# DeltaNet and Fourier mixing on one core: all rounds inverted in 16-token blocks that TensorE joins, MLP activations on ScalarE alone, and a rearranged start

## The chip, the cores and the metric

The kernel runs on one core of a Trainium2 chip. A core has a matrix engine (TensorE, PE in the profile; its weight loads are listed as PEld), a vector engine (VectorE, DVE), an activation engine (ScalarE, ACT), a general engine (GpSimd, POOL) and a queue engine that issues most of the DMAs (SyncE, SP). Matrix products land in PSUM, from which DVE or ACT must copy ("evict") them to SBUF. The metric is the device time of the kernel in microseconds (us).

## The reference

Two blocks, one after the other. The first is a delta rule recurrence over 768 tokens for 4 batches x 8 heads with 48 channels per head; the second mixes each batch's 768 x 384 matrix by a two-dimensional Fourier transform and sends it through a normalised MLP.

```python
k_n = k / (np.linalg.norm(k, axis=-1, keepdims=True) + 1e-06)
for t in range(S):
    kt, vt, bt = (k_n[:, :, t], v[:, :, t], beta[:, :, t, None])
    y[:, :, t] = np.einsum('bhd,bhde->bhe', q[:, :, t], state)
    v_old = np.einsum('bhde,bhd->bhe', state, kt)
    state = state + bt[:, :, :, None] * np.einsum('bhd,bhe->bhde', kt, vt - v_old)
...
x = y.transpose(0, 2, 1, 3).reshape(B, S, H * D)          # 4 x 768 x 384
mixed = np.real(np.fft.fft(np.fft.fft(x, axis=1), axis=2))
u = x + mixed
un = (u - mean(u)) / np.sqrt(var(u) + 1e-06)
out = u + np.maximum(un @ w_ch1, 0.0) @ w_ch2             # 384 -> 1536 -> 384
```

All inputs are float32.

## The kernel before, in words

**Groups, steps and rounds.** The tokens are cut into 24 groups of 128 (`g`; six to a batch), each of two chunks of 64. Inside a chunk the recurrence is turned into matrix products, for which a triangular matrix of the keys' inner products must be inverted. This is done in blocks of 32 tokens, for four groups at a time: a *round* `r` (`RL` = 4), six rounds in all, rounds 0 and 1 for the first eight groups.

**What is done for a group.** `pre_a(g)` transposes the keys and forms the inner products `G` (and `GX` between the two blocks of a chunk). `invert(r)` turns a round's `G` into the inverse: a transpose, a short chain on the diagonal (norms), then an elimination of 31 pairs of DVE instructions (`tmp`, L376, and `M`, L380) over the whole 32 x 32 block of all heads at once, and two more transposes (L383, L384). `pre_q(g)` transposes the queries and forms their products with the keys, masked (`LQ`). `pre_m(g)` joins the two 32-blocks of a chunk on TensorE (`px`, `py`) and makes `WT` and `U0`. `step(g, c)` then advances the recurrence by one chunk: TensorE product, DVE subtraction (`U`, L601), TensorE product, DVE addition (`S`, L620), and after the second chunk the output `x`.

**Two ways to invert.** Rounds 0 and 1 use `invert16`: DVE eliminates only inside 16-token blocks (15 pairs, L453 and L456), and `join(g)` adds the missing corner per group with two sets of small TensorE products. The first set (`py`) needs the untransposed corner of `G`, which POOL copies to `Gc` beforehand (L411); ACT scales it into `Y` (L477), the second set (`pm`) follows, and DVE adds it to the inverse and its transpose (L491). Rounds 2 to 5 use `invert`, without joins.

**After the recurrence.** `fourier(b)` folds the batch (`E`, `O`) and multiplies it by tables (`evt`, `odt`, `dtab`); `mlp(b)` normalises (`un`), transposes, and runs the two matrix products: twelve chunks `ph` of 256 tokens, each evicted to `hT` with a ReLU, alternately by ACT (L769) and DVE (L771), then `po`, added to `x` by DVE (L781) and stored.

**Order of the work.** The engines' order is written out by hand: each function is a generator, and the program advances them piece by piece (`advance`, `part`, `run`). In batch 0 everything is in line: keys of rounds 0 and 1, inversion 0, queries, first joins, then for each group the steps with the next groups' `pre_m`, `join` and `pre_q` in between, inversion 1 and the weights' conversion in pieces (`fill`). From batch 1 on, `run` goes round-robin over one step, the next group's `pre_q` and `pre_m`, the next round's `pre_a` or inversion (24 pieces per step, 6 per turn, in three steps of the eight of a round), and the MLP of the batch before (`side`). SP's queue is not ordered by hand; the framework orders it.

**Spins.** `spin(n)` issues `n` products of a zero tile with itself (`unread<-idle`, L206) that nobody reads. They keep TensorE at work between pieces; there are 80 of them, two records each in the profile.

**Loads.** SP issues nearly all loads. POOL issues those of K and V for groups 0 and 1 and of beta for rounds 0 and 1; ACT issues a table of masks (`pack`) and one group of keys. The Fourier tables are issued before the first join.

Of the kernel before, what the change touches and what calls it, by code (L numbers as in the profile page):

```python
# [9 lines left out]
F32 = mybir.dt.float32  # L10
# [14 lines left out]
def _consts(S, DM):  # L25
# [6 lines left out]
    upper = -1.0 * (p[:, None] % W >= V16)  # L32
    pack = np.concatenate([ident, su, blk, upper], axis=1)
# [27 lines left out]
def kernel(  # L61
# [121 lines left out]
    pack = const.tile([128, 128 + C + 3], F32, name="pack")  # L183
    w2 = const.tile([128, KF, DM], F32, name="w2")

    early = w2.rearrange("p c m -> p (c m)").rearrange("p (n h d) -> p n h d", h=8, d=64)
    nc.vector.memset(early[:, :, :, D:64], 0.0)
# [12 lines left out]
    idle = wk.tile([128, 128], F32, tag="LQ", bufs=2, name="idle")  # L200
    nc.vector.memset(idle, 0.0)  # L201
    unread = []

    def spin(n):
        for _ in range(n):
            nc.tensor.matmul(unread[0][:, 0:128], lhsT=idle, rhs=idle, start=True, stop=True,  # L206
                             skip_group_check=True)
    m_su = pack[:, 128:128 + C]
    m_blk = pack[:, 128 + C:128 + C + 2]
    m_upper = pack[:, 128 + C + 2:128 + C + 3]  # L210
# [116 lines left out]

    def invert(r):

        G = Gs.pop(r)  # L330
        A = wk.tile([128, W, W], F32, tag="A", bufs=2, name="A")
        M = wk.tile([128, W, W], F32, tag="x" if r == 1 else "M", bufs=2 if r == 1 else 1,
                    name="M")
        nc.gpsimd.memset(M, 0.0)
        nc.vector.transpose(A, G.rearrange("p m s -> p s m"))
        yield
        nrm = wk.tile([128, W], F32, tag="nrm", bufs=2, name="nrm")
        bn = wk.tile([128, W], F32, tag="bn", bufs=2, name="bn")
        flat = "p a b -> p (a b)"
        diag = A.rearrange(flat)[:, 0:W * W:W + 1]  # L340

        nc.scalar.activation(nrm, diag, ACT.Sqrt)
        yield
        nc.vector.tensor_scalar(nrm, nrm, 1e-19, None, op0=ALU.max)
        yield
        nc.vector.reciprocal(bn, nrm)
        yield
        nc.vector.tensor_tensor(bn, bn, diag, op=ALU.mult)
        yield
        nc.vector.tensor_tensor(nrm, nrm, bn, op=ALU.add)  # L350
        yield
        nc.vector.reciprocal(bn, nrm)
        yield
        nc.vector.tensor_tensor(bn, bn, diag, op=ALU.mult)
        yield
        nc.vector.scalar_tensor_tensor(nrm, nrm, 0.25, bn, op0=ALU.mult, op1=ALU.add)
        yield
        nc.vector.tensor_scalar(nrm, nrm, 1e-6, None, op0=ALU.add)
        yield
        nT = wk.tile([128, W], F32, tag="nT", bufs=2, name="nT")  # L360
        nc.vector.transpose(nT, nrm)
        nc.vector.tensor_tensor(nrm, nrm, nrm, op=ALU.mult)
        yield
        nc.vector.reciprocal(nrm, nrm)
        yield
        nc.vector.tensor_tensor(bn, nrm, betas.pop(r), op=ALU.mult)
        yield
        nc.vector.scalar_tensor_tensor(A, A, -1.0, bn[:, :, None].broadcast_to([128, W, W]),
                                       op0=ALU.mult, op1=ALU.mult)
        nc.vector.tensor_copy(M.rearrange(flat)[:, 0:W * W:W + 1], bn)  # L370
        yield
        for j in range(W - 1):
            n = W - 1 - j
            t = wk.tile([128, 256], F32, tag="tmp", bufs=2, name="tmp")
            t = t[:, 0:n * (j + 1)].rearrange("p (a b) -> p a b", a=n)
            nc.vector.tensor_tensor(t, A[:, j + 1:W, j:j + 1].broadcast_to([128, n, j + 1]),  # L376
                                    M[:, j:j + 1, 0:j + 1].broadcast_to([128, n, j + 1]),
                                    op=ALU.mult)
            yield
            nc.vector.tensor_tensor(M[:, j + 1:W, 0:j + 1], M[:, j + 1:W, 0:j + 1], t, op=ALU.add)  # L380
            yield

        nc.vector.transpose(A.rearrange("p m t -> p t m"), M)  # L383
        nc.vector.transpose(G.rearrange("p m s -> p s m"), M.rearrange("p t s -> p s t"))  # L384
        rounds[r] = (A, G, nT)
        yield

    Gc = {}

    def invert16(r):  # L390
# [3 lines left out]
        if not Gc:  # L394
            Gc[0] = wk.tile([128, 2, W, W], F32, tag="O", name="Gc")
# [10 lines left out]
        def pairs(t):  # L406
            return t.rearrange("p (e i) -> p e i", e=2)

        A, M, Ad, Md = whole(A2), whole(M2), blocks(A2), blocks(M2)
        nc.gpsimd.memset(M2, 0.0)  # L410
        nc.gpsimd.tensor_copy(Gc[0][:, r], G)  # L411
        yield
# [4 lines left out]
        diag = A2.rearrange("p e f -> p (e f)")[:, 0:W * W:W + 1]  # L417
        ddiag = M2.rearrange("p e f -> p (e f)")[:, 0:W * W:W + 1]
        nc.scalar.activation(nrm, diag, ACT.Sqrt)
        yield  # L420
# [24 lines left out]
                                op=ALU.mult)  # L445
        nc.vector.tensor_scalar(ddiag, bn, -1.0, None, op0=ALU.mult)
        yield
        for j in range(V16 - 1):
            n = V16 - 1 - j
            t = wk.tile([128, 256], F32, tag="tmp", bufs=2, name="tmp")  # L450
            t = t[:, 0:2 * n * (j + 1)].rearrange("p (e a b) -> p e a b", e=2, a=n)
            sh = [128, 2, n, j + 1]
            nc.vector.tensor_tensor(t, Ad[:, :, j + 1:V16, j:j + 1].broadcast_to(sh),  # L453
                                    Md[:, :, j:j + 1, 0:j + 1].broadcast_to(sh), op=ALU.mult)
            yield
            nc.vector.tensor_tensor(Md[:, :, j + 1:V16, 0:j + 1], Md[:, :, j + 1:V16, 0:j + 1], t,  # L456
                                    op=ALU.add)
            yield
        nc.vector.transpose(G.rearrange("p m s -> p s m"), M.rearrange("p t s -> p s t"))
        nc.vector.transpose(A.rearrange("p m t -> p t m"), M)  # L460
# [5 lines left out]
    def join(g):  # L466

        r, li = divmod(g, RL)
        MTd, Md, _ = rounds[r]
        py = ps_one()  # L470
        for m in range(8):
            for q4 in range(4):
                rw = slice(W * q4, W * q4 + V16)
                mm(py[W * q4:W * q4 + W, W * m:W * m + W], Gc[0][rw, r, 8 * li + m, :],
                   Md[rw, 8 * li + m, :], m == 0)
        Y = wk.tile([128, 8, W], F32, tag="QT", bufs=2, name="Y")
        nc.scalar.activation(Y.rearrange("p m s -> p (m s)"), py[:, 0:8 * W], ACT.Copy,  # L477
                             scale=m_upper)
        yield
        pm = ps_one()  # L480
        for m in range(8):
            for q4 in range(4):
                rw = slice(W * q4, W * q4 + W)
                mm(pm[rw, V16 * m:V16 * m + V16], Y[rw, m, :], MTd[rw, 8 * li + m, V16:W], m == 0)
            for q4 in range(4):
                rw = slice(W * q4, W * q4 + W)
                o = 8 * V16 + V16 * m
                mm(pm[rw, o:o + V16], MTd[rw, 8 * li + m, :], Y[rw, m, 0:V16], False)
        for t, s0, o in ((Md, 0, 8 * V16), (MTd, V16, 0)):
            d = t[:, 8 * li:8 * li + 8, s0:s0 + V16]  # L490
# [6 lines left out]
    def pre_q(g, QT=None, LQ=None):  # L497

        Q, KT = home_q(g), KTs.pop(g)
        early = QT is not None  # L500
# [23 lines left out]
        if early:  # L524
            nc.scalar.activation(dst, src, ACT.Copy)
            nc.gpsimd.tensor_tensor(dst, dst, mask, op=ALU.mult)
        else:
            nc.vector.tensor_tensor(dst, src, mask, op=ALU.mult)
        yield

    def pre_m(g):
# [53 lines left out]
        yield  # L585

# [461 lines left out]
```

## Time and profile before

| what | value |
|---|---|
| median of 3 runs (range) | 832.66 us (831.57 to 838.21) |
| the profiled execution's own time | 832.35 us |
| its span, first to last instruction | 830.6 us |
| mean granted clock of TensorE | 0.891 |
| PE busy | 760.7 us, 92%, 12040 matmul records |
| PEld busy | 591.2 us, 71% |
| DVE busy | 387.1 us, 47% |
| ACT busy | 206.9 us, 25% |
| POOL busy | 136.4 us, 16% |

How to read it: a float32 matmul stands in the profile as two records. Busy times of PE are modelled, since matmuls are pipelined, so a PE that is busy all the time can still do more per microsecond: what it does depends on the clock that it is granted and on the size of its tiles. A group line of the profile gives the line of the program, the engine, the operation, the tiles (out<-in), the shape, the number of instructions, then their busy time, the mean of one in ns, the idle time before them and what ended it. "issue" is time in which an engine waited for nothing that the profile shows.

### The profile page before, as it was taken

The numbers are of one execution on the slowest core, as the hardware profiler recorded it, in microseconds if no ns is written. First come the engines' busy times: TensorE is split into PE (matmuls) and PEld (weight loads), VectorE is DVE, ScalarE is ACT, GpSimd is POOL, SyncE is SP. The second block draws the span as 40 slices with busy tenths as digits, with TensorE's granted clock in tenths as the row PEclk, the third lists the DMA queues.
The fourth block names the chain that finished last, engine by engine and source line by source line (L and its number), as shares of the span: only waits on it lengthen the run. The fifth ranks groups of instructions, "written<-read, shape, count | busy, mean of one in ns | idle before, by whom it ended". The sixth has DMA issues, their size and how long they took to land.

```text
span 830.6 us, 26585 instructions
## 1 busy us (share of the span) xinstructions
PE 760.7 (92%) x12040; PEld 591.2 (71%) x12040; DVE 387.1 (47%) x960; ACT 206.9 (25%) x478; POOL 136.4 (16%) x163
## 2 busy tenths in 40 slices
PE   8789999689978899899998998899999999999998
PEld 7678888577746667568876766777768677686774
DVE  2837344647998118944358513599222141521110
ACT  4313332154321323114321222222222111110010
POOL 4821223202321101121100102102000020100000
PEclk9755555596999999989998999999999999889999
DMA  9801223144210322102221122002020000000000
GB/s 152 218 14 32 60 64 98 27 118 110 82 30 21 60 44 42 35 23 41 41 44 24 28 45 45 11 11 45 12 49 17 12 11 1 19 1 20 9 11 19
DMA packets 107459, 36.28 MB, mean 44 GB/s; under 512 B 99633, under 2 KB 102994, under 8 KB 107346
## 3 DMA queue, kind: packets, MB, share of 16 engines
q1 hardware_dynamic: 105266, 33.46, 18.3%
q8 instruction: 94, 1.54, 0.8%
q0 software_dynamic: 896, 0.82, 0.6%
q10 hardware_dynamic: 1184, 0.30, 0.2%
q14 instruction: 19, 0.16, 0.1%
HBM read 29.84 MB, written 4.72 MB: 42 GB/s over the span
## 4 chain that ended last, share of the span: by engine, by line
PE 66%; DVE 22%; issue 4%; POOL 3%; ACT 2%; DMA 2%; SPq 0%; POOLq 0%; DVEq 0%; ACTq 0%
PE ph L106 17%; PE po L106 16%; PE pair L106 11%; PE one L106 8%; DVE M L380 4%; PE unread L206 4%; DVE tmp L376 4%; PE pf L106 3%; PE one L109 3%; PE pb L106 2%; PE ptr L109 1%; DVE A L383 1%; DVE G L384 1%; POOL E L688 1%; POOL E L687 1%
## 5 line engine op out<-in xcount | busy, mean ns | idle before, releaser
L106 PE MATMUL ph<-unT,w 128*128 128x256 f32 x864 | 212.2, 399 | 7.2 <-DVE hT L771 3.9
L106 PE MATMUL po<-w,hT 128*128 128x384 f32 x576 | 199.3, 498 | 6.9 <-POOL w L276 4.2
L106 PEld LDWEIGHTS ph<-unT,w 128*128 128x128 f32 x864 | 165.9, 198 | 35.4 <-DVE hT L771 6.6
L106 PEld LDWEIGHTS po<-w,hT 128*128 128x128 f32 x576 | 108.6, 193 | 76.2 <-POOL w L276 5.4
L771 DVE TENSOR_SCALAR hT<-ph 128x256 f32<-128x256 f32 x72 | 30.3, 421 | 106.7 <-PE ph L106 106.6
L769 ACT ACTIVATE hT<-ph 128x256 f32<-128x256 f32 x72 | 27.7, 384 | 153.5 <-PE ph L106 150.5
L781 DVE TENSOR_TENSOR x<-x,po 128x384 f32<-128x384 f32 x24 | 13.2, 552 | 99.1 <-PE po L106 99.1
L537 POOL TENSOR_TENSOR V<-V,nT 128x384 f32<-128x384 f32 x24 | 21.9, 912 | 186.4 <-DMA V<-in_v_dram 86.0
L541 POOL TENSOR_TENSOR MT<-A,pack 128x512 f32<-128x512 f32 x24 | 24.9, 1045 | 147.6 <-PE one L106 83.3
L206 PE MATMUL unread<-idle 128*128 128x128 f32 x160 | 46.6, 421 | 2.3 <-DVE idle L201 2.3
L106 PE MATMUL one<-V,MT 64*64 64x48 f32 x768 | 47.1, 240 | 0.5 <-ACT MT L565 0.3
L376 DVE TENSOR_TENSOR tmp<-A,M 128x31 f32<-128x31 f32 (+15 forms) x124 | 44.6, 360 | 3.4
L380 DVE TENSOR_TENSOR M<-M,tmp 128x31 f32<-128x31 f32 (+15 forms) x124 | 43.9, 354 | 3.1
L106 PE MATMUL pair<-MT,K 64*64 64x64 f32 x768 | 42.9, 259 | 2.2 <-ACT MT L565 1.7
L106 PEld LDWEIGHTS one<-V,MT 64*64 64x64 f32 x768 | 43.2, 158 | 2.1 <-ACT MT L565 1.1
L106 PEld LDWEIGHTS pair<-MT,K 64*64 64x64 f32 x768 | 38.8, 153 | 5.3 <-issue 2.9
L206 PEld LDWEIGHTS unread<-idle 128*128 128x128 f32 x160 | 33.4, 280 | 5.9 <-DVE idle L201 2.2
L106 PE MATMUL pair<-KT 48*32 48x64 f32 x1536 | 23.1, 237 | 12.3 <-issue 8.1
L620 DVE TENSOR_TENSOR S<-S,pair 128x192 f32<-128x192 f32 x40 | 14.0, 351 | 43.4 <-PE pair L106 43.4
L106 PE MATMUL pb<-dtab,F 97*128 97x97 f32 (+1 forms) x192 | 28.4, 296 | 2.4 <-DVE x L781 2.3
L106 PEld LDWEIGHTS pair<-KT 48*32 48x32 f32 x1536 | 18.2, 112 | 17.0 <-issue 14.3
L601 DVE TENSOR_TENSOR U<-U,pair 128x192 f32<-128x192 f32 x44 | 15.5, 352 | 31.6 <-PE pair L106 31.6
(152 smaller groups left out, 1050.1 us busy)
## 6 DMA issues: line engine op xcount, KB each, us to landing
w<-in_moe_w_ch_dram SPq DMA_DIRECT2D x12, 768.0 KB
out_dram<-x SPq DMA_DIRECT2D x24, 192.0 KB
K<-in_k_dram SPq DMA_DIRECT2D x88, 48.0 KB
V<-in_v_dram SPq DMA_DIRECT2D x88, 48.0 KB
C<-in_k_dram SPq DMA_DIRECT2D x18, 192.0 KB
Q<-in_q_dram SPq DMA_DIRECT2D x18, 192.0 KB
w<-in_q_dram SPq DMA_DIRECT2D x6, 192.0 KB
evt<-k_even SPq DMA_DIRECT2D x1, 579.0 KB
```

The lines of the kernel that those rows point to most:

```text
L106: nc.tensor.matmul(o, lhsT=lhsT, rhs=rhs, start=start, stop=stop, skip_group_check=True)
L109: nc.tensor.matmul(o, lhsT=src, rhs=ident[0:src.shape[0], 0:src.shape[0]], is_transpose=True, start=start, stop=True, skip_group_check=True)
L206: nc.tensor.matmul(unread[0][:, 0:128], lhsT=idle, rhs=idle, start=True, stop=True, skip_group_check=True)
L376: nc.vector.tensor_tensor(t, A[:, j + 1:W, j:j + 1].broadcast_to([128, n, j + 1]), M[:, j:j + 1, 0:j + 1].broadcast_to([128, n, j + 1]), o ...
L380: nc.vector.tensor_tensor(M[:, j + 1:W, 0:j + 1], M[:, j + 1:W, 0:j + 1], t, op=ALU.add)
L537: nc.gpsimd.tensor_tensor(V.rearrange("p c j d -> p (c j) d"), V.rearrange("p c j d -> p (c j) d"), nT[:, m8, None].broadcast_to([128, 8, ...
L541: nc.gpsimd.tensor_tensor(MT, MTd[:, m8, None, :].broadcast_to([128, 8, 2, W]), m_blk[:, None, :, None].broadcast_to([128, 8, 2, W]), op=A ...
L601: nc.vector.tensor_tensor(U.rearrange("p (jj jp) e -> p jp jj e", jp=2), U.rearrange("p (jj jp) e -> p jp jj e", jp=2), pw[:, :, 0:2 * D]. ...
L620: nc.vector.tensor_tensor(s1v, s0.rearrange("p h j e -> p h (j e)"), pk, op=ALU.add)
L769: nc.scalar.activation(hT[:, fc, :], ph, ACT.Relu)
L771: nc.vector.tensor_scalar(hT[:, fc, :], ph, 0.0, None, op0=ALU.max)
L781: nc.vector.tensor_tensor(x[:, T, :], x[:, T, :], po, op=ALU.add)
```

## The change

- `invert16` becomes the only `invert` and serves all six rounds; the 32-token elimination goes. The corner of the inner products no longer needs a copy on POOL: ACT writes it into the empty corner of `M`, the transpose that makes `G` carries it along, and DVE clears the corner again before the other transpose.
- `join` takes that corner from the inverse's own tile. Its first set of products has 16 columns where it had 32; `Y` becomes one constant tile whose other half stays zero; a second ACT pass removes the corner from the tile again. From group 8 on, `prepare(g)` runs `join(g)` ahead of `pre_m(g)`: three of its five pieces in a group's first step and two in the second.
- The inversion is spread over three steps as 17 pieces per step, 4 per turn.
- `mlp` evicts all twelve chunks with ACT.
- `pre_q` of the first six groups masks on DVE as it evicts, where ACT evicted and POOL masked.
- `idle` is cleared ahead of `early`. K and V of groups 0 and 1 are issued by SP, ahead of the queries, where POOL issued them. The Fourier tables are issued after the first group's steps, the keys of groups 8 to 10 and the queries of groups 6 and 7 after the second group's.
- `spin` puts up to four products into one instruction of up to 512 columns. There are 106 spins where there were 80, of which 50 where there were 33 in batch 0's loop, and 20 in a row before the first join where there were 8.
- In the first stage inversion 0 and `pre_q(0)` are drained among the keys, all other `pre_q` do their first half before the first join, and the first joins are drained one after the other. The start of inversion 2 and the first `prepare` move ahead of batch 1.

```diff
     def spin(n):
-        for _ in range(n):
-            nc.tensor.matmul(unread[0][:, 0:128], lhsT=idle, rhs=idle, start=True, stop=True,
+
+        while n > 0:
+            k4 = min(n, 4)
+            rhs = idle if k4 == 1 else idle[:, None, :].broadcast_to([128, k4, 128])
+            nc.tensor.matmul(unread[0][:, 0:128 * k4], lhsT=idle, rhs=rhs, start=True, stop=True,
                              skip_group_check=True)
+            n -= k4
...
+    Ypad = const.tile([128, 8, W], F32, name="Y")
+    nc.gpsimd.memset(Ypad, 0.0)
...
         nc.gpsimd.memset(M2, 0.0)
-        nc.gpsimd.tensor_copy(Gc[0][:, r], G)
-        yield
         nc.vector.transpose(A, G.rearrange("p m s -> p s m"))
...
         nc.scalar.activation(nrm, diag, ACT.Sqrt)
+
+        nc.scalar.activation(M[:, 0:V16, V16:W], A[:, 0:V16, V16:W], ACT.Copy)
...
         nc.vector.transpose(G.rearrange("p m s -> p s m"), M.rearrange("p t s -> p s t"))
+        yield
+        nc.vector.memset(M[:, 0:V16, V16:W], 0.0)
         nc.vector.transpose(A.rearrange("p m t -> p t m"), M)
...
         for m in range(8):
             for q4 in range(4):
                 rw = slice(W * q4, W * q4 + V16)
-                mm(py[W * q4:W * q4 + W, W * m:W * m + W], Gc[0][rw, r, 8 * li + m, :],
-                   Md[rw, 8 * li + m, :], m == 0)
-        Y = wk.tile([128, 8, W], F32, tag="QT", bufs=2, name="Y")
-        nc.scalar.activation(Y.rearrange("p m s -> p (m s)"), py[:, 0:8 * W], ACT.Copy,
-                             scale=m_upper)
+                mm(py[W * q4:W * q4 + W, V16 * m:V16 * m + V16], Md[rw, 8 * li + m, :],
+                   Md[rw, 8 * li + m, 0:V16], m == 0)
+        Y = Ypad
+        nc.scalar.activation(Y[:, :, 0:V16], py[:, 0:8 * V16].rearrange("p (m s) -> p m s", s=V16),
+                             ACT.Copy, scale=m_minus)
+        nc.scalar.activation(Md[:, m8, V16:W], Md[:, m8, V16:W], ACT.Copy, scale=m_second)
...
-        if early:
-            nc.scalar.activation(dst, src, ACT.Copy)
-            nc.gpsimd.tensor_tensor(dst, dst, mask, op=ALU.mult)
-        else:
-            nc.vector.tensor_tensor(dst, src, mask, op=ALU.mult)
+        nc.vector.tensor_tensor(dst, src, mask, op=ALU.mult)
...
+    def prepare(g):
+        if g >= 2 * RL:
+            yield from join(g)
+        yield from pre_m(g)
...
-                if fc % 2:
-                    nc.scalar.activation(hT[:, fc, :], ph, ACT.Relu)
-                else:
-                    nc.vector.tensor_scalar(hT[:, fc, :], ph, 0.0, None, op0=ALU.max)
+                nc.scalar.activation(hT[:, fc, :], ph, ACT.Relu)
...
-                pq, pm = pre_q(g + 1), pre_m(g + 1)
+                pq, pm = pre_q(g + 1), prepare(g + 1)
...
-                live.append((part(pm, 1 + c), 1))
+                live.append((part(pm, 3) if c == 0 else pm, 1))
...
-                    live.append((part(inv, 24), 6))
+                    live.append((part(inv, 17), 4))
...
-                load_kv(0, nc.gpsimd)
-                load_beta(1, nc.gpsimd)
...
+        load_beta(1, nc.gpsimd)
+        load_kv(0)
         for g in range(1, 4):
             load_q(g)
-        load_kv(1, nc.gpsimd)
+        load_kv(1)
...
-        nc.sync.dma_start(out=evt, in_=cn["even"].ap())
-        nc.sync.dma_start(out=odt, in_=cn["odd"].ap())
-        nc.sync.dma_start(out=dtab, in_=cn["dtab"].ap())
-        for g in range(2 * RL, 2 * RL + 3):
-            load_c(g)
-        load_q(NL)
-        load_q(NL + 1)
-        for qg in qs[1:4]:
+        for qg in qs[1:]:
             spin(2)
             advance(qg)
-            spin(2)
-            drain(qg)
-        spin(8)
+        spin(2)
+        drain(qs[1])
+        spin(20)
...
+            if g == 0:
+                nc.sync.dma_start(out=evt, in_=cn["even"].ap())
+                nc.sync.dma_start(out=odt, in_=cn["odd"].ap())
+                nc.sync.dma_start(out=dtab, in_=cn["dtab"].ap())
+            if g == 1:
+                for i in range(2 * RL, 2 * RL + 3):
+                    load_c(i)
+                load_q(NL)
+                load_q(NL + 1)
```

## The prediction

> **What bounds the kernel now.** I read the page's shares and slices first, then busy time by stage, then the groups, then what TensorE (PE) itself waits for, and last the order of time.
>
> ```profile
> span 830.6 us, 26585 instructions
> PE 760.7 (92%) x12040; PEld 591.2 (71%) x12040; DVE 387.1 (47%) x960; ACT 206.9 (25%) x478; POOL 136.4 (16%) x163
> ...
> DVE  2837344647998118944358513599222141521110
> ...
> PEclk9755555596999999989998999999999999889999
> ```
>
> PE is busy for 92% of the span, so the question in each stage is what PE would do faster. From slice 3 to slice 8 (about 40 to 160 us) its granted clock is half. VectorE (DVE) shows four humps of 8 to 9 tenths after that: the inversions of rounds 2 to 5.
>
> ```profile
> 66.60:156.00 89.40, 80.04 (x2266) 69.48 (x2264) 43.46 (x82) 27.71 (x51) 25.26 (x21) 0.54 0.28 64
> ...
> 219.30:255.60 36.30, 31.43 (x279) 20.97 (x278) 34.67 (x81) 8.92 (x15) 9.35 (x7) 1.00 0.20 51
> ...
> 323.30:341.00 17.70, 17.00 (x310) 14.04 (x309) 16.88 (x53) 4.57 (x11) 1.17 (x2) 1.00 0.23 42
> ...
> 438.50:472.50 34.00, 29.91 (x431) 23.39 (x430) 26.12 (x66) 6.10 (x14) 3.98 (x4) 0.85 0.14 28
> ...
> 538.00:583.50 45.50, 42.94 (x353) 33.17 (x352) 40.57 (x114) 10.38 (x29) 4.78 (x8) 1.00 0.11 25
> 583.50:727.30 143.80, 139.58 (x1817) 104.92 (x1816) 41.71 (x110) 30.18 (x75) 13.06 (x15) 0.98 0.07 17
> ```
>
> Columns: stretch, its length, busy time of PE, weight loads, DVE, ScalarE (ACT) and POOL, granted clock, DMA share, GB/s. The first row is batch 0's recurrence: PE busy 80 of 89 us at a clock of 0.54. The next four hold the inversions: DVE 34.7 of 36.3 us, 16.9 of 17.7, 26.1 of 34, 40.6 of 45.5, yet PE is busy 121.3 of these 133.5 us too. The last has no inversion and PE leaves only 4.2 us open. So relief on DVE alone can give little, and work added to PE costs nearly its price.
>
> **The inversions (rounds 2 to 5).**
>
> ```profile
> L376 DVE TENSOR_TENSOR tmp<-A,M 128x31 f32<-128x31 f32 (+15 forms) x124 | 44.6, 360 | 3.4
> L380 DVE TENSOR_TENSOR M<-M,tmp 128x31 f32<-128x31 f32 (+15 forms) x124 | 43.9, 354 | 3.1
> L456 DVE TENSOR_TENSOR M<-M,tmp 128x30 f32<-128x30 f32 (+7 forms) x30 | 12.1, 403 | 0.9
> L453 DVE TENSOR_TENSOR tmp<-A,M 128x30 f32<-128x30 f32 (+7 forms) x30 | 8.2, 272 | 1.0
> L771 DVE TENSOR_SCALAR hT<-ph 128x256 f32<-128x256 f32 x72 | 30.3, 421 | 106.7 <-PE ph L106 106.6
> L769 ACT ACTIVATE hT<-ph 128x256 f32<-128x256 f32 x72 | 27.7, 384 | 153.5 <-PE ph L106 150.5 <-issue 3.0
> ```
>
> A 32-token round costs DVE (44.6 + 43.9)/4 = 22.1 us in its elimination; a 16-token round (12.1 + 8.2)/2 = 10.2 us. With the scaling (1.41 us against 0.69) and one small memset more, DVE is rid of some 12.4 us in each of four rounds, 50 us in all. What of it returns to the span is what PE waits for there: G (L384) 4.8 us, hT (L771) 3.9 + 2.6, x (L781) 3.0 + 2.3, the copy at L370 0.9, S (L620) 3.1 outside batch 0, and the converted weights (L276, themselves behind DVE) 4.2: 24.8 us together. I take 21 back; the ends are 10 (the 12.2 us that PE leaves open in the four stages, less what its other waits keep) and 25.
>
> **The joins.** Groups 8 to 23 now need one join each, 16 more. Each is 32 matmuls of 16 columns and 64 more, two records each: 192 records. At the full clock (97.2 us) groups of eight such records start 64 ns apart, 8 ns each: 1.54 us, and two more changes of tile shape at about 0.15 us: 1.85 us, or 29.6 us for 16. If they fell wholly into PE's gaps the cost would be near 8 us, so that is the low end. They also eat instructions fast:
>
> ```profile
> PE one L106 <- issue: 7.4, 7, 1.6
> PE one L106 <- DVE G L384: 4.8, 3, 1.8
> ```
>
> Six of the seven "issue" waits lie inside the eight joins there are now (45.8, 97.8, 115.1, 136.3 us among them): PE has nothing to issue for about 1 us each. Between the long matmuls of the MLP this should be rarer; I take 3 us for the 16, ends 0 and 15. Each join also adds two ACT passes (the 128x256 form at L477 took 474 ns; these are half as wide) and two DVE additions of 288 ns, 9 us on a DVE that has just lost 50. The wait is new for what stands behind it: the first product of `pre_m` now stands behind the join's DVE addition, but a piece of the MLP (1.3 us) lies between them in the round-robin; in the step where a round ends it does not, and this is in the 3 us. Net of batches 1 to 3: 29.6 + 3 - 21 = **+11.6**, ends -10 and +35.
>
> **MLP activations on ScalarE.** 72 evictions of 421 ns leave DVE (their waits are counted above) and come to ACT at 384 ns. The cover is PE's own chunk: 72 records of `ph` take 15.81 us in the last stage, 1.3 us for each eviction's chunk. ACT is 25% busy. Taken at 0; if ACT were late with half a microsecond in every sixth, +6.
>
> [...]
>
> **The start.** DVE's chain for round 0 runs from 16.7 to 38.3 us. Two of its additions took 1.76 and 1.55 us in place of 0.27, each beside a POOL pass (the LQ mask, 1.28 us; the memset and the copy of G, 1.0 and 1.05). Both kinds of pass go or move: the mask becomes one DVE pass of 686 ns, the copy of G a corner of M by one ACT pass. So -2.8 us, +0.9 for DVE's new passes. PE lost 1.5 and 3.35 us to "issue" at 21.6 and 26.8 us, with the DMA engines 87% busy. Against that, 16 loads of K and V move from POOL's queue (0.62 us each) to SP's (0.75 each): Q1 to Q3 stand behind 8 of them and leave 6 us later, Q4 and Q5 behind all 16 and 12 us later than now (by 17.2 us), and PE wanted Q1 at 31.3. The 32 spins before the first join (20 now) take 12 x 0.216 = 2.6 us more, beside the wait for round 0. Join 0 starts at 41.7 us; I say 4.5 us earlier, ends -8 and +3. Three spins less among the first joins: -1. The earlier memset of `idle` only starts spins sooner (first useful matmul at 6.0): 0. Tables, later C and later Q: SP's queue does not follow the program (the beta loads of line 983 left at 40.7 us, loads of line 980 after 65), so they may leave early all the same: 0, ends -2 and +2; evt is first needed near 160.
>
> **The clock in batch 0's loop.**
>
> ```profile
> 93.30:96.70 3.40, 3.40 (x82) 3.08 (x75) 1.97 (x2) 1.72 (x3) 2.63 (x2) 0.50 0.76 233
> 96.70:100.10 3.40, 2.05 (x150) 1.86 (x148) 0.00 (x0) 0.98 (x2) 0.00 (x0) 1.00 0.31 57
> 100.10:103.50 3.40, 3.40 (x82) 2.86 (x84) 2.27 (x5) 0.32 (x1) 0.20 (x1) 0.50 0.23 40
> ```
>
> The clock changes at multiples of 3.4 us. I counted for each such stretch the share of the array that its matmuls fill (tile area times columns; 216 ns for a full 256-column record as in `ph`, so 6% for one spin). After stretches of 0.40 and more the clock is full, below 0.28 it is half, and between it goes both ways: the first row holds 0.31 and is followed by the full clock; the second, a join, holds 0.12 and loses it. A group of the loop fills 1.27 stretches now and takes five (0.25 on average). With nine spins in place of five or six it fills 1.36, and the densest run (spin, last part of `pre_m`, spin, output) rises from 0.34 to 0.35. That is close to the edge from below; once at full clock a group could take 12 us, 3.5 stretches of 0.39, which just holds it. A full-clock stretch does 150 records where a half-clock one does 82, so each is worth up to 2.8 us; I use 2.4. Eleven more of the loop's 26 (two now): -26. Seventeen more spins at 0.216 us: +4. **-22**, ends -40 (clock held throughout) and +7 (none; 17 spins at 0.43).
>
> [...] The slices contradict busy time as the measure: PE is fully busy from 60 to 80 us at 0.5. [...]
>
> **Sum**, against the profiled execution's own 832.35 us (span 830.6; the median of the runs is 832.66): -4.5 - 1 - 22 + 11.6 = -15.9, so **817 us**; own range 803 to 826.
>
> **The rivals.**
> 1. **PE pays for the joins and the clock stays half: slower.** Place: batches 1 to 3. For it: PE is 90% busy even where DVE is the hump, and six joins of eight stalled on issue. Against: 24.8 us of waits on DVE. Price: 29.6 + 8 - 21 = +16.6, start -5.5, loop +4 (half of 17 spins at 0.43): **848**. It decides from fewer than four more full-clock stretches, each 2.4 us, with the joins as I took them.
> 2. **The edits cancel.** Five or six stretches rise (-13, spins +4), the joins cost +13, the start gives 4: **832**. For it: the shares in the loop lie on both sides of the edge.
> 3. **The change does not do what it says at the start:** tables leave early all the same, Q comes late behind the K and V loads, and join 0 starts 3 us later: the forecast's 817 becomes 825.
>
> **How the numbers follow.** Forecast with its variant 3: 0.46; slower: 0.34; cancelled: 0.20. About 1% can be told from no change here (the three runs spread by 0.8%). Faster by over 1% (under 824.3): 0.46; within: 0.20; slower: 0.34. The 80% range leaves out the ends at which everything goes one way: 797 to 850.
>
> **What would show it.** Right: a PEclk mean above 0.7 in batch 0's loop with that loop 20 us shorter; DVE under 7 tenths in the four humps; PE's waits for G, hT and x mostly gone; 16 joins of 1.8 to 2.5 us in batches 1 to 3. Wrong: PEclk still 5 from 40 to 160 us; issue waits in most of the new joins; batches 1 to 3 more than 20 us longer; PE waiting for ACT at `ph`.

## The result and the profile after

The changed kernel takes **873.67 us** (median of 4 runs, 867.51 to 876.14) against 835.43 us for the kernel before on the same chip: a ratio of 1.0447, 95% interval 1.0364 to 1.0529. It is slower, and slower than the forecast's whole range. The profiled execution took 872.1 us, 39.8 us more than the one of before.

The page after, in the same parts as before: shares, then busy tenths of VectorE and the granted clock by slice.

```profile
span 870.3 us, 32636 instructions
...
PE 793.1 (91%) x15060; PEld 605.6 (70%) x15060; DVE 319.3 (37%) x804; ACT 243.0 (28%) x590; POOL 116.1 (13%) x140
...
DVE  2744535556961018526137112386112123320000
...
PEclk9965755687999999998998999999999999979999
```

VectorE did lose 68 us of work, and its humps have shrunk to one slice each (9, 8, 7 and 8 tenths), not to under 7 tenths as forecast. TensorE got 32 us more work and 3020 more records, and the span follows TensorE. The clock still stands at 5 to 7 tenths in slices 3 to 8.

To see where the time went I took the ends of the stages from the trace: the last state update of batch 0's loop, and ScalarE's copies `Q` of the Fourier mix, of which the last one closes batch 0 and the first one of each later batch shows that its steps are done. After minus before: +1.0 at the end of the loop (162.4 against 161.4 us), +0.4 where batch 0 ends (216.7 against 216.3), then +13.6, +30.9 and +39.7 where batches 1, 2 and 3 have done their steps, and +39.8 at the end. So start and loop together brought nothing, and batches 1 to 3 lost everything. First batch 0's loop and the three batch stages after, then the same three stages before (columns as in the prediction):

```profile
66.60:156.00 89.40, 79.45 (x2276) 62.89 (x2271) 41.68 (x90) 25.43 (x51) 15.05 (x12) 0.58 0.26 61
216.70:395.40 178.70, 166.35 (x3501) 125.40 (x3502) 77.64 (x186) 53.77 (x133) 29.99 (x29) 0.97 0.19 40
395.40:589.90 194.50, 183.80 (x3854) 141.50 (x3853) 75.34 (x208) 57.16 (x149) 21.43 (x25) 0.94 0.15 31
589.90:751.90 162.00, 160.49 (x2976) 122.53 (x2975) 40.03 (x110) 43.50 (x112) 16.62 (x20) 1.00 0.09 21
```

```profile
216.30:381.90 165.60, 149.87 (x2216) 109.64 (x2215) 100.71 (x249) 41.49 (x95) 28.99 (x27) 0.96 0.19 42
381.90:559.10 177.20, 165.62 (x2703) 127.49 (x2702) 96.79 (x262) 46.68 (x116) 20.28 (x24) 0.96 0.17 33
559.10:712.30 153.20, 149.64 (x2013) 113.27 (x2012) 51.40 (x134) 33.43 (x83) 15.73 (x19) 1.00 0.09 21
```

VectorE gives up 23, 21 and 11 us in the three stages; TensorE's busy time grows by 16, 18 and 11, and the stages by 13, 17 and 9. What TensorE waits for, after:

```profile
PE one L106 <- issue: 12.3, 10, 2.8
PE pair L106 <- issue: 9.6, 7, 2.5
PE ptr L109 <- DVE un L708: 9.5, 1, 9.5
PE one L106 <- DVE G L444: 5.6, 3, 2.9
PE pair L106 <- DVE S L573: 4.9, 2, 4.7
PE ph L106 <- ACT hT L721: 4.1, 5, 1.1
```

The waits for hT of VectorE are gone, and those for x (L731) are 2.4 us where they were 5.3. The wait for G has stayed and has changed its cause: L444 is the join's addition. In place of the others stand more "issue" (21.9 us in these two lines, 17 times), one new wait of 9.5 us, and 4.1 us for ScalarE. In the kernel before the same two lines had 16.1 us, 14 times; the prediction shows one of them, this is the other:

```profile
PE pair L106 <- issue: 8.7, 7, 3.3
```

### The profile page after: what moved, and what is told of

The parts are those of the page before. It is cut to its first block, busy times and chain, and to the rows that moved or that the text cites. A ratio compares the mean times of both kernels' runs of the same rounds, so it can differ in the third digit from the quotient of the medians.

```text
span 870.3 us, 32636 instructions
## 1 busy us (share of the span) xinstructions
PE 793.1 (91%) x15060; PEld 605.6 (70%) x15060; DVE 319.3 (37%) x804; ACT 243.0 (28%) x590; POOL 116.1 (13%) x140
## 4 chain that ended last, share of the span: by engine, by line
PE 73%; DVE 12%; issue 5%; SPq 3%; ACT 3%; POOL 2%; DMA 1%; POOLq 0%; ACTq 0%; DVEq 0%
PE ph L106 20%; PE po L106 20%; PE pair L106 11%; PE one L106 10%; PE pf L106 4%; PE unread L209 3%; PE one L109 2%; PE pb L106 2%; SPq L138 2%; DVE tmp L401 1%; PE ptr L109 1%; DVE M L404 1%; SPq L148 1%; POOL w L281 1%; DVE A L358 1%
## 5 line engine op out<-in xcount | busy, mean ns | idle before, releaser
L106 PE MATMUL ph<-unT,w 128*128 128x256 f32 x864 | 217.6, 404 | 6.4 <-ACT hT L721 4.1
L721 ACT ACTIVATE hT<-ph 128x256 f32<-128x256 f32 x144 | 54.9, 383 | 144.3 <-PE ph L106 144.2
L731 DVE TENSOR_TENSOR x<-x,po 128x384 f32<-128x384 f32 x24 | 13.3, 552 | 157.3 <-PE po L106 157.3
L209 PE MATMUL unread<-idle 128*128 128x256 f32 (+2 forms) x108 | 50.5, 572 | 1.9 <-DVE idle L188 1.0
L554 DVE TENSOR_TENSOR U<-U,pair 128x192 f32<-128x192 f32 x44 | 15.5, 351 | 83.7 <-PE pair L106 77.8
L106 PE MATMUL one<-A,Y 32*32 32x16 f32 x1536 | 36.3, 187 | 6.8 <-issue 6.8
L603 DVE TENSOR_TENSOR x<-x,pair 128x384 f32<-128x384 f32 x24 | 13.3, 554 | 72.9 <-ACT x L594 55.8
L106 PEld LDWEIGHTS one<-A,Y 32*32 32x32 f32 x1536 | 33.1, 116 | 7.7 <-issue 7.2
L106 PE MATMUL one<-Y,A 32*32 32x16 f32 x1536 | 35.2, 189 | 3.4 <-issue 2.7
L106 PEld LDWEIGHTS one<-Y,A 32*32 32x32 f32 x1536 | 31.5, 115 | 6.1 <-issue 4.1
L502 ACT ACTIVATE XM<-one 32x256 f32<-32x256 f32 x48 | 18.0, 375 | 58.7 <-PE one L106 58.1
L106 PE MATMUL pair<-S,WT 48*64 48x48 f32 x704 | 22.8, 245 | 9.5 <-DVE S L573 4.7
```

The lines of the kernel that those rows point to most:

```text
L106: nc.tensor.matmul(o, lhsT=lhsT, rhs=rhs, start=start, stop=stop, skip_group_check=True)
L209: nc.tensor.matmul(unread[0][:, 0:128 * k4], lhsT=idle, rhs=rhs, start=True, stop=True, skip_group_check=True)
L502: nc.scalar.activation(XM[rw].rearrange("p m s -> p (m s)"), px[rw, 0:8 * W], ACT.Copy, scale=-1.0)
L554: nc.vector.tensor_tensor(U.rearrange("p (jj jp) e -> p jp jj e", jp=2), U.rearrange("p (jj jp) e -> p jp jj e", jp=2), pw[:, :, 0:2 * D]. ...
L603: nc.vector.tensor_tensor(xv, xv, pl[:, :, 0:4 * D], op=ALU.add)
L721: nc.scalar.activation(hT[:, fc, :], ph, ACT.Relu)
```

## The experiments

All twelve kernels are changes of the kernel before or of the changed one. "Stage" means one of the three batch stages above, cut at the same events in each kernel; "time at half clock" is summed from the granted-clock record of the trace.

### The join and the relief, apart

**e1_relief**: the kernel before with the 16-token inversion in rounds 2 to 5 and no joins there (so the corner of each 32-token block is left out of the result).

```
-    A = wk.tile(...); for j in range(W - 1): ...      # 32 tokens, 31 steps
+    invert(r) of the changed kernel                   # 16 tokens, 15 steps
-    live.append((part(inv, 24), 6))
+    live.append((part(inv, 17), 4))
```

> The kernel before with rounds 2 to 5 inverted in 16-token blocks (17 pieces per step, 4 per turn) and without their joins: the corner of each 32-token inverse is left out. It measures what relief of VectorE alone gives back. Theory A (TensorE is the bound of batches 1 to 3, its gaps are only partly VectorE's): 2 to 9 us less than before, 825 to 832. Theory B (the recorded term, 21 us of waits return): about 812. Either way VectorE's busy time falls by some 50 us.

Measured: 825.27 us against 831.32, ratio 0.9953 [0.9912, 0.9994]. The three stages took 157.4, 174.3 and 152.6 us: 8.2, 2.9 and 0.6 less than before, 11.7 in all. That is as Theory A had it.

**e2_both**: the same, with the joins of groups 8 to 23.

```
+    def prepare(g):
+        if g >= 2 * RL:
+            yield from join(g)
+        yield from pre_m(g)
```

> The kernel before with rounds 2 to 5 inverted in 16-token blocks and joined by TensorE as in the changed kernel; start, spins, loads and the MLP's evictions as before. Theory A: this part is the whole loss, 868 to 876. If the ScalarE evictions or the new start carry a part of the 40 us, it stays below 860.

Measured: 875.28 us, ratio 1.0623 [1.0545, 1.0702]. Stages 181.0, 190.1 and 166.9 us: +15.4, +12.9, +13.7, together 42.0. The inversions and joins alone, on the kernel before, make a loss as large as the whole.

**e3_price**: the kernel before with its 32-token inversions, and the joins' 96 matmuls in groups 8 to 23 beside them, into a PSUM tile that nobody reads.

```
+    for m in range(8): ... mm(py[...], Md[rw, 8 * li + m, :], Md[rw, 8 * li + m, 0:V16], m == 0)
+    for m in range(8): ... mm(pm[rw, ...16 columns], MTd[...], Md[...], m == 0) ... mm(pm[...], Md[...], MTd[...], False)
```

> The kernel before with 32-token inversions, and in groups 8 to 23 the join's 96 matmuls issued at the join's places into PSUM that nobody reads: no ScalarE pass, no VectorE addition, nobody waits for them. The price on TensorE alone. Theory A (price of the instructions themselves, 2.3 to 2.8 us for each of 16): 870 to 880. Theory C (the chain of the join, that is ScalarE, VectorE and the wait in front of the next product, makes the loss): below 850, since the records alone are 1.54 us by 16.

Measured: 886.79 us, ratio 1.0720 [1.0635, 1.0805]. Stages +19.8, +15.5, +17.6: 52.9 us, or 3.3 us for a join on which nothing depends. That is above Theory A's range. e2 less e1 gives 53.7 us for the same joins when they are used. So TensorE's own work makes nearly all of the cost. The chain through ScalarE and VectorE (Y, the two additions) is not free, though: in e2 TensorE waits twice for the joins' addition, in batches 1 and 2:

```profile
PE one L107 <- DVE G L549: 4.3, 2, 2.9
```

With the half clock put apart (27.3 us more of it in e3 than before, 17.1 more in e2 than in e1, at the 0.37 worked out below) the used joins cost 47.4 us and the unread ones 42.8, a difference of about these 4.3 us. Relief (-11.7) and joins (+53) add up.

**e7_half**: e3 with the same array work in half as many instructions.

```
-    for m in range(8): ... 16 columns each
+    for m in range(4): ... 32 columns each
```

> The kernel before with unread matmuls of the joins' array work in groups 8 to 23, as in e3_price, but half as many instructions, each with twice the columns (48 matmuls of 32 columns in place of 96 of 16 per group). Theory A (the price is one of instructions: records issued at 8 ns each, and instructions fetched in bursts): the 51 to 55 us that e3_price cost fall to about half, 25 to 30, so 857 to 862 us. Theory B (the price is the array's time and the change of tile shape): the cost stays, 880 us and more.

Measured: 853.13 us, ratio 1.0282 [1.0210, 1.0355]: 22 us over its kernel before, where e3 was 55 over. Here the price goes with the number of instructions and not with the array work. (The pages count as many weight loads as matmuls, 12040 of each in the kernel before, so these are halved too: the run does not tell the two apart.) Part of it shows in TensorE's "issue" waits of the three stages, first of before, then of e3_price, then of e7_half:

```profile
PE pair L106 <- issue: 2.4, 4, 1.8
PE ph L106 <- issue: 0.8, 1, 0.8
PE one L109 <- issue: 0.7, 1, 0.7
```

```profile
PE one L106 <- issue: 7.1, 8, 1.8
PE pair L106 <- issue: 5.0, 4, 3.0
```

```profile
PE pair L106 <- issue: 2.9, 3, 1.4
PE one L106 <- issue: 1.3, 1, 1.3
```

3.9, 12.1 and 4.2 us. With 192 records to a join these waits are 8 us longer than before, with 96 they are 0.3 us longer. The changed kernel has 11.7 us there. Most of it stands before products of `pair` (9.6 us of the 11.7). Of these, 7.8 us are five waits before the keys' products of `pre_a`, which come behind a join; in a join there is one wait, of 2.1 us.

Beside these waits stands the DMA queue that the page lists as `instruction`, with packets of 16 KB. In the kernel before and in the changed one (packets, MB, share of 16 engines):

```profile
q8 instruction: 94, 1.54, 0.8%
```

```profile
q8 instruction: 118, 1.93, 0.9%
```

Both have about 256 matmul and weight-load records to a packet (24080 to 94, 30120 to 118); e3_price has 118 packets as well, e7_half 106. On average they come 7 to 9 us apart. In the fourteen traces (before, after and the twelve runs), from 30 us on, TensorE has 152 "issue" waits of over 0.5 us, and 141 of them end 1.2 to 1.6 us after such a packet has ended (10 of 10 in the kernel before, 11 of 12 in the changed one). That they are waits for the fetch of instructions is my reading of this; the profile names nothing that they wait for.

### The rest of the change

**e4_after32**: the changed kernel with 32-token inversions and no joins in rounds 2 to 5 (and one buffer of `tmp` in place of two).

```
-        if g >= 2 * RL:
-            yield from join(g)
         yield from pre_m(g)
-    inv = invert(r + 1)
+    inv = invert32(r + 1)
```

> The changed kernel with rounds 2 to 5 back on 32-token inversions (24 pieces per step, 6 per turn) and no joins there; its start, spins, loads, masks and ScalarE evictions stay. Theory A: all of the loss goes, 826 to 836, and the rest of the change is worth nothing either way. If the rest costs, 840 and more; if the rest gains what the prediction had for start and clock (27 us), 805.

Measured: 847.24 us, ratio 1.0263 [1.0198, 1.0328]. Without any new join the change still costs 2 to 3%. Its profile is level with before up to the end of batch 0 (+0.3), then +9.7 in the first stage, -4.1 in the second, +7.3 in the third. Three further parts can make this: ScalarE's activations, the spins, and the opening of round 2.

**e5_act**: the kernel before with all activations of the MLP on ScalarE.

```
-                if fc % 2: nc.scalar.activation(hT[:, fc, :], ph, ACT.Relu)
-                else: nc.vector.tensor_scalar(hT[:, fc, :], ph, 0.0, None, op0=ALU.max)
+                nc.scalar.activation(hT[:, fc, :], ph, ACT.Relu)
```

> The kernel before, with one edit of the change alone: all 144 activations of the MLP's first product on ScalarE. Theory A (the forecast's term, 0): TensorE's own chunk of 1.3 us covers ScalarE's 384 ns, and 36 more of VectorE's 421 ns passes are gone from each batch, so nothing or a little is gained: TensorE's waits for VectorE at hT (6.5 us in the trace of before) vanish, 825 to 832 us, with no waits for ScalarE above 2 us. [...]

Measured: 837.81 us, ratio 1.0097 [1.0058, 1.0136]: about 1% slower, above Theory A's 825 to 832. ScalarE is not late (TensorE waits 0.7 us for its hT). The one profile is ahead until 568 us, by 6.0 us at 522 and still by 1.5 there. It loses 7.4 us in the next 22, most of which ran at half clock although TensorE was busy:

```profile
564.80:585.20 20.40, 19.84 (x204) 16.38 (x203) 8.73 (x28) 4.35 (x11) 3.08 (x6) 0.50 0.15 33
```

Over the three stages this execution has 54.6 us at half clock, before has 27.3.

**e6_alt**: the changed kernel with the alternating activations back (the reverse of that diff).

> The changed kernel with the activations of the MLP back on VectorE and ScalarE in turn. Theory A: the edit is worth nothing or little in the changed kernel, and its loss is the joins': 868 to 876 us. Theory B: ScalarE alone is what makes batches 1 to 3 late on top of the joins (it has the join's two passes more as well): 860 us or less, and TensorE's waits for ACT at hT (4.1 us in the changed kernel) are gone.

Measured: 876.11 us, ratio 1.0549 [1.0478, 1.0619], which overlaps the changed kernel's own interval. So Theory A: in the changed kernel this part neither costs nor brings what can be told.

**e8_nospin**: the changed kernel without the 50 unread passes of batch 0's loop.

```
-                spin(2)      # and the others of the loop
+                spin(0)
```

> The changed kernel without the spins of batch 0's loop (nine unread 128-column passes per group left out). Theory A (the spins do release the clock in the loop, and their own time and the new waits eat the gain): the loop's granted clock falls from 0.58 to 0.5, and S10, the loop's end, comes 4 us later or more (166 us or later). Theory B (the spins do nothing for the clock, they are only extra work): the clock stays within 0.02 of 0.58 and the loop ends 3 to 6 us earlier (156 to 159 us).

Measured: one run, 860.27 us. The loop ends at 150.4 us, 12.0 earlier than in the changed kernel. Neither theory holds as it was written: the clock of the window fell to 0.54, and the gain is twice that of Theory B. **e10_nosb** takes the 33 passes out of the kernel before.

> The kernel before with the spins of batch 0's loop left out (five or six unread 128-column passes per group). If spins release no clock there and are plain work (as e8_nospin has it, which ended the loop 12 us earlier than the changed kernel): loop 5 to 8 us shorter, 823 to 827 us. If the few that there were held part of the clock: the loop's two or three full-clock stretches go, and the time is 831 us or more.

Measured: 823.02 us, ratio 0.9915 [0.9879, 0.9951]; its loop ends at 152.9 us, 8.5 earlier, as the first reading had it. Net of what it releases, a pass costs 0.24 us in the one and 0.26 in the other. **e12_spinb4** does each of the 33 four times.

```
-                spin(1)
+                spin(4)
```

> The kernel before with every spin of batch 0's loop done four times (20 to 24 per group). Theory A (a large enough share of the array filled releases the clock, and the forecast only had too few spins for it): of the 89 us from 66.6 us on at least half is at full clock, mean above 0.75, and S10 comes no later than 166 us. Theory B (spins do not raise the clock here, or not enough): the clock stays under 0.65 and S10 comes 25 to 40 us later, 186 us or more.

Measured: 836.81 us, ratio 1.0030 [0.9981, 1.0079]; its loop ends at 164.2 us, 2.8 later than before. The same window of batch 0's loop, in e10_nosb, then e8_nospin, then e12_spinb4:

```profile
66.60:156.00 89.40, 64.72 (x2240) 59.30 (x2238) 47.79 (x93) 28.54 (x52) 27.62 (x23) 0.50 0.27 65
```

```profile
66.60:156.00 89.40, 63.47 (x2251) 58.67 (x2243) 46.40 (x99) 25.72 (x51) 19.65 (x16) 0.54 0.27 63
```

```profile
66.60:156.00 89.40, 81.34 (x2418) 73.33 (x2417) 39.47 (x75) 25.91 (x47) 22.88 (x20) 0.84 0.26 61
```

The clock rises with the passes, and Theory A of e12 holds: 0.84 with 132 passes (0.41 of the window's array filled), against 0.54 with 33 (0.21) and 0.50 with none (0.15). From 41.7 us to the end of the loop the time at half clock fell from 109.1 to 55.2 us. But 99 more passes at 0.216 us (two records of 128 columns; in the trace of before, `ph` records of 256 columns start 216 ns apart at full clock) are 21 us, and the loop ended 2.8 us later, so 54 us less of half clock must have brought some 18 (a difference, not a measurement): it nearly cancels. With 50 passes (the changed kernel, 0.58) little is released, and they are paid nearly in full.

**e9_block**: the changed kernel with the opening of round 2 back behind the hand-ordered stretch.

```
-        inv = invert(2)
-        advance(inv)
-        drain(pre_q(NL))
-        pm = prepare(NL)
-        advance(pm)
+    inv = invert(2)                     # after the `with`
...
+                pm = prepare(NL)        # in b == 0, ahead of drain(pm)
+                drain(pre_q(NL))
```

> The changed kernel with one part taken back: the work that opens round 2 and group 6 (invert, pre_q, pre_m) stands again after the hand-ordered stretch and not at its end. Theory A (in the changed kernel TensorE stands idle from 187.3 to 196.8 us, where the kernel before did 324 records of group 6, because the hand order puts these behind the pieces of fourier(0) and of the MLP): the idle time shrinks to under 3 us, and the end comes 7 to 9 us earlier, 863 to 868 us. Theory B (the idle time is VectorE's and ends with its chain whoever stands where): 871 us or more.

Measured: 863.64 us, ratio 1.0400 [1.0339, 1.0462]. The wait has gone. The order of time around it in the changed kernel (start, length, engine; in brackets the idle time before):

```profile
185.78 1.50 PE L106 MATMUL pb<-dtab,F 96*128 96x96 f32 x12
...
190.56 1.80 POOL L281 TENSOR_TENSOR w<-wtmp 128x768 f32<-128x768 f32 x1 [11.09 <-DVE wtmp L278]
190.99 1.59 DVE L686 TENSOR_TENSOR x<-x,Q 128x193 f32<-128x193 f32 x1
...
196.15 0.87 DVE L708 TENSOR_SCALAR un<-x,mv,rstd 128x384 f32<-128x384 f32 x2 [0.92 <-POOL rstd L696]
196.77 1.51 PE L109 MATMUL ptr<-pack,un 128*128 128x128 f32 x6 [9.49 <-DVE un L708]
```

TensorE stands from 187.3 to 196.8 us while VectorE adds the Fourier mix to x, normalises it and converts weights between. In the kernel before, the same VectorE chain ran, but TensorE worked on group 6 meanwhile (`one<-pack,Q`, `G,GX`, `A,XM`, the state's first products, 185.0 to 195.3 us), because there the framework placed this work, and not the hand-written order. At the end of the hand-ordered stretch this work comes at 219 us and later. In e9_block TensorE waits 1.7 us there in place of 9.5; the stretch from the loop's end to the end of the first batch stage shrinks by 8.5 us (233.0 to 224.5). The timed intervals of the two kernels overlap, so the size rests on these two profiles. e4_after32, which keeps the opening at the end of the hand order, agrees: with its half clock put apart at the 0.37 worked out below, its three stages are 8.4 us longer, 1.6 shorter and 1.0 longer than before.

**e11_back**: the changed kernel with 32-token inversions and no new joins, alternating activations, the opening of round 2 behind the hand order, and no spins in the loop (and one buffer of `tmp`, as in e4); the new start, the late tables and batch 0's order stay.

> The changed kernel with its four costly parts taken back: 32-token inversions without joins in rounds 2 to 5, alternating activations, the opening of round 2 after the hand order, and no spins in batch 0's loop; the new start, the late tables and batch 0's order stay. If the costs add up (e4_after32 847, less 8 for the opening, less 10 to 12 for the spins): 825 to 829 us, a little under the kernel before. If another part of the change still costs (the late loads, batch 0's order): 835 us or more.

Measured: **820.31 us** (12 runs), ratio 0.9855 [0.9817, 0.9894]. It is under the 825 to 829 us expected and beats both kernels: by the profile 10 us ahead of before at the end of the loop (151.4 us), the same 10 at the end of batch 0, 13.6 at the end. e10_nosb, one edit on the kernel before, has most of it.

## Why the prediction was wrong, step by step

**The start, -4.5: right in kind, half in size, then lost.** Join 0 began at 39.5 us, 2.1 earlier. The long additions are gone (none over 0.29 us). But the LQ mask, now on VectorE, stood in front of the inversion's square root chain and waited 2.4 us for TensorE's product. That wait, with a whole chain queued behind it, was not in the sum. By the loop's first state update nothing was left (67.8 against 67.7 us).

**The clock in the loop, -22: the term that failed most.** That a fuller array goes with a higher clock was right (0.41 filled and 0.84 in e12, 0.21 and 0.54 before); the step that failed is "eleven more of the loop's 26 stretches at full clock". From 41.7 us to the end of the loop the time at half clock fell by 8 us only, 109.1 to 100.9, little more than two stretches of 3.4. The fault was to forecast full clock from a share that stayed under 0.40, with hope in one dense run. The share was read too high as well: by the records of the traces it is 0.21 in the window from 66.6 to 156 us, not 0.25, and rose to 0.23, not 0.27. And a stretch was taken for worth 2.4 us, from a row at full clock whose 150 records are a join's, much smaller than the 82 of the rows beside it. e12 has some 0.34 us for each us of half clock, batches 1 to 3 have 0.37 (below), so a stretch of 3.4 is worth some 1.2 us. The price of the spins was about right: I took 4 us for 17; 33 cost 8.5 and 50 cost 12.0, so 17 cost 3.5 net of what they release. The start and the loop's other edits gave back 2.5 us (the loop ends 108.7 us after 41.7 in e8, 111.2 in e10), hence the +1.

On the measure: TensorE is busy for 80.0, 79.5 and 81.3 of these 89.4 us in before, after and e12, at clocks of 0.54, 0.58 and 0.84. In the kernel before it is busy without a break at half clock here:

```profile
60.00:80.00 20.00, 20.00 (x590) 18.07 (x582) 13.61 (x32) 6.67 (x14) 3.10 (x3) 0.50 0.14 27
```

So busy time does not tell the three kernels apart; filled array does: 0.21, 0.23 and 0.41 of this window, and 0.15 in e8 and e10. Counted as in the prediction over all stretches of 3.4 us of the fourteen traces, each of the 2525 that held 0.40 or more was followed by full clock, and each of the 364 under 0.20 by half, although TensorE was busy for over 98% of the time in 73 of them; of the 541 between, 190 were followed by full. (In the trace of before alone it is 175 of 175 and 24 of 24, in that of the changed kernel 184 of 184 and 24 of 24.) The prediction's two bounds hold in the trace of before; over all traces the lower one is 0.20, not 0.28.

**Joins 29.6, stalls 3, relief -21: all the loss.** A join that met no stall took what I said: 64 records in 0.66 us and 128 in 1.19, 1.85 us. But sixteen joins cost 52.9 us alone (e3), or 3.3 us each. The stalls were too small: issue waits took 8 us more than before, not 3, and in the changed kernel the joins' addition, which was to be in these 3, makes TensorE wait another 5.1 us in batches 1 to 3. A further part had no term at all: the clock of batches 1 to 3. The third stage is the same program of 2012 records in before, e10_nosb and e12_spinb4 (before is above at 153.20 us and a clock of 1.00):

```profile
544.70:704.40 159.70, 156.53 (x2013) 119.59 (x2012) 50.95 (x133) 33.45 (x83) 15.71 (x19) 0.95 0.09 20
```

```profile
560.10:718.20 158.10, 154.93 (x2013) 118.23 (x2012) 50.88 (x134) 33.51 (x83) 15.74 (x19) 0.96 0.09 20
```

17.1 and 13.7 us at half clock made it 6.5 and 4.9 us longer: 0.37 us for each. e3 has 27.3 us more of it than before in the three stages, 10 us. The remainder, 52.9 - 29.6 - 8.2 - 10.1 = 5, I could not place. Whether joins make half clock likelier is not shown: the three stages hold 20.5 to 54.6 us of it in the seven kernels without new joins and 27.3 to 54.6 in the seven with joins or their copies. The relief was 11.7 us by the profile, 9.2 with the half clock put apart, and 4 to 6 in timed runs: at or under my low end of 10, not 21. With G out of the way, TensorE waited for hT and x instead, 8.3 and 6.6 us in e1 where it had been 6.5 and 5.3.

**The opening of round 2: the step I did not price.** The diff moves five lines into the hand-ordered stretch. I counted their work as unchanged and did not ask who would fill TensorE's idle time at 187 us without them. By the profiles of e9 and of the changed kernel it cost 8.5 us.

**ScalarE alone, 0:** held in the changed kernel, with 4.1 us of waits for ScalarE where I had 0 to 6. On the kernel before, taking turns was better by 1% (e5_act, ratio 1.0097), though ScalarE's evictions were not late (0.7 us of waits). Whether the edit really makes half clock likelier there, or whether that profile was an unlucky one, stays open.

**The sum for batches 1 to 3**, the clock put apart at 0.37: joins +42.8 (52.9 - 10.1), relief -9.2 (11.7 by the profile, 6.8 us less of half clock taken out), opening of round 2 +7.2 (its share in the first stage), the changed kernel's own 6.8 us more of half clock +2.5, ScalarE -2.0 (e6's stages are 7.1 us longer, 13.7 us more of half clock taken out). That is +41.3 against +39.2 seen. The sum is good to some 7 us only: with e2 for the joins and the relief together (42.0, less 3.8 for its 10.2 us more of half clock) in place of e3 and e1 it is +45.9. Rival 1 had direction, place and cause right, and stopped at 848 because it priced a join at 2.35 us with stalls, kept the relief at 21, and had no term for the opening. Of the signs set out ahead, "PEclk still 5" and "batches 1 to 3 more than 20 us longer" came true, and PE waited for ACT at `ph` (4.1 us). Issue waits in most of the new joins did not: of the seven over half a microsecond in batches 1 to 3, one was in a join and five behind one.

## What to carry to other kernels

Where one engine is busy for 90% of a stage, as TensorE was here, and an edit moves work to it, try a copy of that work, unread, before building the real thing: the copy cost 52.9 us here, the used joins 53.7. Price small matmuls by their number before their columns (e3 lost 55 us, e7, with half as many of twice the columns, 22), and count the stalls that they leave for the instructions behind them (7.8 of 11.7 us in the changed kernel). When lines move into a stretch whose order is fixed by hand, look up in the trace which idle time they used to fill (8.5 us here).

## What the runs showed of the hardware that was not expected

192 records in a row cost 3.3 us a time where 8 ns each makes 1.54; 96 records of twice the columns, the same array work, cost 1.4 us (22 us over 16 groups). An execution's luck with the clock was worth as much as some of the edits here: the same stage took 153.2, 158.1 and 159.7 us with 0, 13.7 and 17.1 us at half clock, and the kernel before ran between 821 and 840 us. The clock of the loop rose from 0.50 without filler passes (e10) to 0.84 with 132 (e12), and these cost more than they brought: the loop ended at 152.9 us without them and at 164.2 with 132. In fourteen traces, 3.4 us with 0.40 or more of the array filled were followed by full clock 2525 times of 2525, with less than 0.20 by half 364 times of 364, in 73 of them with TensorE busy for over 98% of the time. TensorE's "issue" waits of over 0.5 us, from 30 us on, ended 1.2 to 1.6 us after a 16 KB packet of instructions, 141 times of 152.
